# Linear attention and routed experts on one core: state products regrouped on TensorE, the state scaled on ScalarE, small routing operations on GpSimd, weights fetched at a later step

## The chip, the core and the metric

The kernel runs on one core of a Trainium2 chip. A core has five engines that run their own instruction queues in order: TensorE (PE, with weight loads shown as PEld), VectorE (DVE), ScalarE (ACT), GpSimd (POOL) and SyncE (SP), which here only issues transfers. The metric is the device time of one execution in microseconds. The kernel before took 322.28 us as the median of three runs (320.68, 322.28, 323.75).

## The reference

Two layers in a row. The first is a linear attention with a decayed state: batch 4, 8 heads, 768 positions, head size 48.

```python
def _attn_ref(q, k, v, alpha):
    state = np.zeros((B, H, D, D))
    for t in range(S):
        state = alpha[:, :, t, :, None] * state + np.einsum('bhd,bhe->bhde', k[:, :, t], v[:, :, t])
        y[:, :, t] = np.einsum('bhd,bhde->bhe', q[:, :, t], state)
```

Its output, 3072 rows of 384, goes through a mixture of 8 experts with one expert for each row:

```python
def _moe_ref(x, w_skip, w_gate, w1, w2):
    do_compute = x @ w_skip > 0
    logits = x[do_compute] @ w_gate
    e_idx = argmax(logits); gate_w = softmax(logits)[e_idx]
    for e in range(8):
        h = np.maximum(xc[e_idx == e] @ w1[e], 0.0)      # 384 -> 1024
        y[e_idx == e] = gate_w * (h @ w2[e])             # 1024 -> 384
    out[do_compute] = xc + y
```

## The kernel before

**Stage one** walks over 24 tiles of 128 positions: tile i is chunk i // 4 of batch i % 4, with all 8 heads (`static_path`, the loop at L829). In this document *step i* is one turn of that loop. Nothing reorders what the loop writes: each engine runs its instructions in the order of the Python code, and a list of small routing operations (`self.small`) is let out one at a time by `tick()` at fixed places.

Heads are held in pairs: p is the pair (0 to 3), h the half. Half 0 lies on partitions 0 to 47, half 1 on 64 to 111. A tile's work:

- `decay` (L248) for tile i+4: two scans on DVE (`sfx`, `pfx`), then three multiplications on POOL (`total`, keys by `sfx`, queries by `pfx`).
- `scores` (L270) and `causal` (L281) for tile i+1: key-query products on PE into `ps_s`, and a predicated copy by DVE into `st`. `ps_s` has one buffer, so the scores of the next step wait for this copy.
- `turn_k` (L286) for tile i+1: keys transposed on PE, copied to `kt` by ACT.
- `inter` (L296): the old state times the queries; `intra` (L324): values times `st`, added in the same PSUM tiles `ps_y`. There are two such tiles, one for each half, and two ACT copies of 48 partitions bring them to `xt`.
- `outer` (L309): the old state (by an identity product, L315) plus keys times values in `ps_v`; `carry` (L337): DVE multiplies by `total` and writes the new state, which tile i+4 reads.
- `rows` (L348) for tile i-1: PE turns `xt` to rows with the nine routing products; ACT copies `x`, DVE sums the logits.
- Routing. `route_expert` (L379) works on groups of tiles, (0,6), (6,12), (12,15), (15,18), and `route_one` on single tiles from 18 on; `route_rank` counts positions on PE, `route_slot` (L441) makes slot numbers, and `scatter` (L505) writes row numbers and gates to DRAM lists with one indirect transfer for each tile, issued by POOL.

In the same loop the weights of the first expert are fetched in eight pieces (`weight_pieces(0)` from step 3, one piece a step) and split into two parts of lower precision, twelve pieces, one a step, from step 7 (`split_pieces`, L530): ACT makes the high part, DVE or POOL (`n % 5 in (1, 3)`) the low part. The pieces of expert 1 follow from step 18.

**Stage two** runs the eight experts one after the other: gather of its 256 rows, two products with three terms each (`up`, `down`), and an indirect write of the result, while the next experts' weights are fetched and split.

Of the kernel before, what the change touches and what calls it, by code (L numbers as in the profile page):

```python
# [23 lines left out]
P = 128  # L24
# [25 lines left out]
DECAY_MIN = 1e-18  # L50
EG = 8


class Kernel:
# [130 lines left out]
    def attention_pools(self, st):  # L185
# [8 lines left out]
        self.ps_y = [st.enter_context(tc.tile_pool(name=f"ps_y{h}", bufs=1, space=PSUM)) for h in range(2)]  # L194
# [24 lines left out]
        for t in self.xtb:  # L219
            nc.scalar.copy(out=t.rearrange("p a t -> p (a t)"), in_=self.zero)  # L220
# [4 lines left out]
    def warm_up(self, n):  # L225

        ps = self.ps_y[0].tile([P, P], F32, name="ps_y")
        zero = self.nc.const_aps.tensor(0.0, [P, P], F32)
        for _ in range(n):
            self.nc.tensor.matmul(ps, lhsT=zero, rhs=zero, start=True, stop=True)  # L230
# [64 lines left out]

    def inter(self, i):  # L296


        nc, w = self.nc, self.work[i]
        w["y"] = [pool.tile([P, NP, P], F32, name="ps_y") for pool in self.ps_y]  # L300
        state = self.state[i % B][i // B % 2]
        if i // B > 0:
            for p in range(NP):
                for h in range(2):
                    r = slice(64 * h, 64 * h + D)
                    nc.tensor.matmul(w["y"][h][r, p, :], lhsT=state[r, p, :], rhs=w["qh"][r, p, :],  # L306
                                     start=(p == 0), stop=False)

    def outer(self, i):  # L309

        nc, w = self.nc, self.work[i]
        if i // B < C - 1:
            w["pv"] = self.ps_v.tile([P, NP, D], F32, name="ps_v")
            if i >= B:
                nc.tensor.matmul(w["pv"][:PD], lhsT=self.ident[:PD, :PD], rhs=self.state[i % B][i // B % 2][:PD],  # L315
                                 start=True, stop=False)
            for p in range(NP):
                for h in range(2):
                    o = (2 * p + h) * D
                    r = slice(64 * h, PD if h else 64)  # L320
# [3 lines left out]
    def intra(self, i):  # L324

        nc, w = self.nc, self.work[i]
        ps, v = w["y"], w["v"]
        for p in range(NP):
            for h in range(2):
                o = (2 * p + h) * D  # L330
                nc.tensor.matmul(ps[h][64 * h:64 * h + D, p, :], lhsT=v[:, o:o + D],  # L331
                                 rhs=w["st"][:, h, p * P:(p + 1) * P], start=(i < B and p == 0), stop=(p == NP - 1))
        xt = self.xtb[i % 2]
        for h in range(2):
            r = slice(64 * h, 64 * h + D)
            nc.scalar.copy(out=xt[r], in_=ps[h][r])  # L336
# [686 lines left out]
```

## Time and profile before

| | |
|---|---|
| median of three runs | 322.28 us |
| the profiled execution's own time | 324.01 us |
| its span, first to last instruction | 322.3 us |
| mean granted clock of TensorE | 0.936 |
| busy: PE, DVE, ACT, POOL | 291.1, 231.3, 155.1, 140.2 us |
| stage one, to the first expert's first product | about 170 us |
| stage two | about 150 us |

A profile gives, for each engine, when it was busy, and for each idle stretch what ended it. Matmuls overlap in the array, so the sum of their single times is far above the time that a group of them takes; the length of a group is read from the chain of waits or the timeline. "x16" for eight products means that each float32 product is two passes. A PE that is busy all the time may still be waiting inside, and a granted clock below 1.00 means that the array ran slower in that stretch.

### The profile page before, as it was taken

To read this page: it belongs to the slowest core of one execution; us is meant where nothing else is said; L and a number is where in the kernel's file an instruction comes from. 1 tells how busy PE (TensorE), PEld (TensorE's weight loads), DVE (VectorE), ACT (ScalarE), POOL (GpSimd) and SP (SyncE) were. 2 spreads that over 40 slices of the span, in tenths; PEclk is the share of its full clock that TensorE was granted. 3 is DMA by queue.
4 is the path that set the end of the run, shared out by engine and by line. 5 is a ranking of instruction groups with operands and counts; after the bars stand their busy time and mean duration, and the time that the engine had idled before them with its cause. 6 is when DMAs were issued, how large, how long until landed. Compare 5 with 4: busy or idle time off the path is not lost.

```text
span 322.3 us, 7348 instructions
## 1 busy us (share of the span) xinstructions
PE 291.1 (90%) x2816; PEld 269.1 (83%) x2816; DVE 231.3 (72%) x480; ACT 155.1 (48%) x300; POOL 140.2 (44%) x168
## 2 busy tenths in 40 slices
PE   5849799999999869979879889999999999999990
PEld 5748688888887758768779789999999999999990
DVE  8997757899699999975568547776676768685410
ACT  6022324345345415325525449686859596573200
POOL 5174533668965777882472522131413041221111
PEclk9575869999999999978979999999999999999997
DMA  7999899999999977743262568887885868370000
GB/s 236 288 231 158 113 219 235 241 255 221 233 164 225 252 134 153 142 82 78 81 190 60 190 250 274 280 297 248 274 297 179 315 176 287 149 258 17 19 23 24
DMA packets 28123, 60.79 MB, mean 189 GB/s; under 512 B 7110, under 2 KB 14065, under 8 KB 28080
## 3 DMA queue, kind: packets, MB, share of 16 engines
q1 hardware_dynamic: 22960, 50.43, 60.5%
q10 hardware_dynamic: 2176, 4.72, 4.8%
q0 software_dynamic: 2944, 5.09, 4.8%
q8 instruction: 24, 0.39, 0.5%
q14 instruction: 19, 0.16, 0.2%
HBM read 52.96 MB, written 8.89 MB: 192 GB/s over the span
## 4 chain that ended last, share of the span: by engine, by line
PE 75%; issue 5%; DMA 4%; POOL 4%; DVE 3%; ACT 1%; POOLq 0%; SPq 0%; DVEq 0%
PE ps_o L640 20%; PE ps_h L624 19%; PE ps_s L277 7%; PE ps_g L358 7%; PE ps_y L331 6%; PE ps_y L306 5%; PE ps_k L291 3%; PE ps_v L321 3%; DMA xr<-out_dram,meta 2%; PE ps_x L604 1%; PE ps_v L315 1%; DMA xs<-idg,slot 1%; POOL xs L508 1%; DMA meta<-xs 1%; POOL qka L268 1%
## 5 line engine op out<-in xcount | busy, mean ns | idle before, releaser
L645 POOL DMA_INDIRECT out_dram<-o,meta x16 | 16.9, 1058 | 98.8 <-DVE o L643 98.8
L277 PE MATMUL ps_s<-qka 48*128 48x128 f32 x384 | 32.6, 317 | 15.1 <-POOL qka L268 4.5
L277 PEld LDWEIGHTS ps_s<-qka 48*128 48x128 f32 x384 | 27.8, 218 | 20.4 <-issue 6.4
L640 PE MATMUL ps_o<-w2h,hh 128*128 128x384 f32 x128 | 43.8, 342 | 0.0
L336 ACT COPY xt<-ps_y 48x512 f32<-48x512 f32 x48 | 27.9, 581 | 32.1 <-PE ps_y L331 26.7
L640 PE MATMUL ps_o<-w2l,hh 128*128 128x384 f32 x128 | 43.3, 338 | 0.0
L640 PE MATMUL ps_o<-w2h,hl 128*128 128x384 f32 x128 | 43.2, 337 | 0.0
L624 PE MATMUL ps_h<-xh,w1h 128*128 128x256 f32 x192 | 33.9, 283 | 0.0
L624 PE MATMUL ps_h<-xh,w1l 128*128 128x256 f32 x192 | 33.7, 282 | 0.0
L643 DVE SCALAR_TENSOR_TENSOR o<-ps_o,meta,xr 128x384 f32<-128x384 f32 x16 | 9.9, 618 | 32.7 <-PE ps_o L640 26.6
L624 PE MATMUL ps_h<-xl,w1h 128*128 128x256 f32 x192 | 33.2, 282 | 0.0
L629 DVE SCALAR_TENSOR_TENSOR hl<-ps_h,hh 128x512 fp32r<-128x512 f32 x32 | 22.0, 688 | 14.4 <-ACT hh L628 13.0
L284 DVE COPY_PREDICATED st<-mask,ps_s 128x1024 f32<-128x1024 uint8 x24 | 31.2, 1301 | 1.2 <-PE ps_s L277 0.4
L267 POOL TENSOR_TENSOR qka<-qka,sfx 112x512 f32<-112x512 f32 x22 | 28.0, 1271 | 9.2 <-DVE sfx L257 8.9
L546 DVE TENSOR_TENSOR w2l<-raw,w2h 128x512 fp32r<-128x512 f32 x45 | 29.0, 683 | 3.1 <-ACT w2h L542 3.1
L331 PE MATMUL ps_y<-st,vt 128*48 128x128 f32 x384 | 30.6, 297 | 0.0
L358 PE MATMUL ps_g<-xw,xt 112*128 112x105 f32 x184 | 28.6, 303 | 2.1 <-ACT xt L336 2.1
L265 DVE TENSOR_TENSOR_SCAN pfx<-qka,seed 112x512 f32<-112x512 f32 x24 | 29.3, 1220 | 0.7
L546 DVE TENSOR_TENSOR w1l<-raw,w1h 128x512 fp32r<-128x512 f32 x46 | 29.7, 683 | 0.0
L628 ACT ACTIVATE hh<-ps_h 128x512 fp32r<-128x512 f32 x32 | 19.1, 595 | 21.2 <-PE ps_h L624 20.7
L257 DVE TENSOR_TENSOR_SCAN sfx<-qka,seed 112x512 f32<-112x512 f32 x24 | 29.0, 1210 | 0.3
L358 PEld LDWEIGHTS ps_g<-xw,xt 112*128 112x128 f32 x184 | 24.8, 209 | 5.3 <-ACT xt L336 2.3
(148 smaller groups left out, 621.3 us busy)
## 6 DMA issues: line engine op xcount, KB each, us to landing
raw<-in_w_dram SPq DMA_DIRECT2D x64, 384.0 KB
qka<-in_qka_dram SPq DMA_DIRECT2D x36, 288.0 KB
vt<-in_v_dram SPq DMA_DIRECT2D x24, 192.0 KB
out_dram<-x SPq DMA_DIRECT2D x24, 192.0 KB
alpha<-in_nat_dram ACTq DMA_DIRECT2D x8, 576.0 KB
qka<-in_first_dram SPq DMA_DIRECT2D x4, 672.0 KB
out_dram<-xr SPq DMA_DIRECT2D x5, 192.0 KB
qka<-in_first_dram SPq DMA_DIRECT2D x2, 448.0 KB
```

What stands on the lines that cost most here:

```text
L257: nc.vector.tensor_tensor_scan(flat(sfx)[:, ::-1], a[:, 1:SW + 1][:, ::-1], seed[:, ::-1], 0.0, ALU.mult, ALU.max)
L265: nc.vector.tensor_tensor_scan(flat(pfx), a[:, 0:SW], seed, 0.0, ALU.mult, ALU.max)
L267: pool.tensor_tensor(w["kh"][:PD], w["kh"][:PD], sfx[:PD], ALU.mult)
L277: nc.tensor.matmul(ps[:, h, p * P:(p + 1) * P], lhsT=kh[r, p, :], rhs=qh[r, p, :], start=True, stop=True)
L284: self.nc.vector.copy_predicated(w["st"], self.mask, w["ps"])
L331: nc.tensor.matmul(ps[h][64 * h:64 * h + D, p, :], lhsT=v[:, o:o + D], rhs=w["st"][:, h, p * P:(p + 1) * P], start=(i < B and p == 0), sto ...
L336: nc.scalar.copy(out=xt[r], in_=ps[h][r])
L358: nc.tensor.matmul(pg[:, p, :], lhsT=w["xt"][:PD, p, :], rhs=self.xw[:PD, p, :], start=True, stop=True)
L546: eng.tensor_tensor(lo[:, s], raw[:, s], hi[:, s].bitcast(F32), ALU.subtract)
L624: nc.tensor.matmul(ps[:, u, :], lhsT=a[:, k, f * P:(f + 1) * P], rhs=b[:, k, :], start=(n == 0), stop=(n == len(order) - 1))
L629: nc.vector.scalar_tensor_tensor(out=hl, in0=ps, scalar=0.0, in1=hh.bitcast(F32), op0=ALU.max, op1=ALU.subtract)
L640: nc.tensor.matmul(ps, lhsT=a[:, f, js], rhs=b[:, f, :], start=(n == 0), stop=(n == 3 * FT - 1))
```

## The change

- `inter` and `intra` put all heads in one PSUM tile of two banks. Bank h holds half h; within it, two pairs share columns and pair j of the two writes partitions 64j and up. The products are issued in the order (h, j) = (0,0), (1,1), (0,1), (1,0). Those of j = 0 are 64 columns wide, so that partitions 48 to 63 are written too. One ACT copy of 112 partitions replaces the two of 48. The order of heads in the inputs is rearranged to fit (`layouts`).
- `outer` issues its identity product as two, one for each half of the output.
- `carry` is four ACT multiplications of 112x48, each with its column of `total`, in place of one DVE operation.
- In `route_expert`, `d` and the multiplication by `rev` go from DVE to POOL, with one more tick behind the second; `cnt` is added up on POOL for all groups. `route_slot` makes the slots of groups on POOL.
- In the loop, `rows`, `logits` of tile i-1 and `carry` come behind `intra`, and `turn_k` runs one step earlier, at the end of step i for tile i+2.
- `weight_pieces(0)` starts at step 9 (`W0`), its split at step 12; expert 1's first four pieces are fetched at steps 18 to 21, the other four behind the loop.

```diff
+W0 = 9
...
+    HEADS = [(a, h, j) for a in range(NP // 2) for h, j in ((0, 0), (1, 1), (0, 1), (1, 0))]
+
+    def y(self, i, a, h, j):
+        m = D if j else 64
+        return m, self.work[i]["y"][64 * j:64 * j + m, h, a * P:(a + 1) * P]
...
-            for p in range(NP):
-                for h in range(2):
-                    r = slice(64 * h, 64 * h + D)
-                    nc.tensor.matmul(w["y"][h][r, p, :], lhsT=state[r, p, :], rhs=w["qh"][r, p, :],
-                                     start=(p == 0), stop=False)
+            for a, h, j in self.HEADS:
+                r, p = slice(64 * h, 64 * h + D), 2 * a + j
+                m, y = self.y(i, a, h, j)
+                nc.tensor.matmul(y, lhsT=state[r, p * D:p * D + m], rhs=w["qh"][r, p, :], start=(a == 0), stop=False)
...
-                nc.tensor.matmul(w["pv"][:PD], lhsT=self.ident[:PD, :PD], rhs=self.state[i % B][i // B % 2][:PD],
-                                 start=True, stop=False)
+                for r in part:
+                    nc.tensor.matmul(w["pv"][r], lhsT=self.ident[:PD, r], rhs=self.state[i % B][i // B % 2][:PD],
+                                     start=True, stop=False)
...
-        for h in range(2):
-            r = slice(64 * h, 64 * h + D)
-            nc.scalar.copy(out=xt[r], in_=ps[h][r])
+        nc.scalar.copy(out=xt[:PD].rearrange("p (a h) t -> p h a t", h=2),
+                       in_=w["y"][:PD, :, :2 * P].rearrange("p h (a t) -> p h a t", t=P))
...
-            nc.vector.tensor_tensor(self.state[i % B][(i // B + 1) % 2][:PD], w["pv"][:PD],
-                                    total[:PD].to_broadcast([PD, NP, D]), ALU.mult)
-            self.tick()
+            new = self.state[i % B][(i // B + 1) % 2]
+            for p in range(NP):
+                nc.scalar.mul(out=new[:PD, p, :], in_=w["pv"][:PD, p, :], mul=total[:PD, p, :])
...
+        nc.gpsimd.tensor_tensor(d, L, bc(mx), ALU.subtract)
         yield nc.vector.tensor_tensor(eq, L, bc(mx), ALU.is_equal)
-        nc.vector.tensor_tensor(d, L, bc(mx), ALU.subtract)
         nc.scalar.activation(out=ex, in_=d, func=AF.Exp)
-        yield nc.vector.tensor_tensor(eq, eq, bc(self.rev), ALU.mult)
+        yield nc.gpsimd.tensor_tensor(eq, eq, bc(self.rev), ALU.mult)
+        yield
...
-            (nc.gpsimd if g1 < SOLO else nc.vector).tensor_tensor(self.cnt[:, i + 1, :], self.cnt[:, i, :], self.m[:, i, :], ALU.add)
+            nc.gpsimd.tensor_tensor(self.cnt[:, i + 1, :], self.cnt[:, i, :], self.m[:, i, :], ALU.add)
...
-        yield nc.vector.tensor_scalar(out=self.slot[:, g0:g1, :], in0=s2, scalar1=BIG, scalar2=None, op0=ALU.add)
+        eng = nc.vector if n == 1 else nc.gpsimd
+        yield eng.tensor_scalar(out=self.slot[:, g0:g1, :], in0=s2, scalar1=BIG, scalar2=None, op0=ALU.add)
...
-                if i == 3:
+                if i == W0:
                     fetch = self.weight_pieces(0)
-                if i == 18:
+                if i == W0 + 9:
                     fetch = self.weight_pieces(1)
-                advance(fetch, 1)
+                if W0 <= i < W0 + 13:
+                    advance(fetch, 1)
...
-                if i == 7:
+                if i == W0 + 3:
                     split = self.split_pieces(0, early=True)
```

What the new order of the loop makes of the queues, at the places that the prediction speaks of. First TensorE in step 5, before (`qka_129` holds tile 6, `qka_134` tile 5, `xt_158` tile 4):

```order
L277 MATMUL ps_s<-qka_129 128x128 x8
L291 MATMUL ps_k<-ident,qka_129 128x112 x4
L306 MATMUL ps_y<-qka_134,state_153 48x128 x8
L358 MATMUL ps_g<-xw,xt_158 128x105 x4
L315 MATMUL ps_v<-state_153,ident 112x192
L321 MATMUL ps_v<-vt,kt 64x48
L321 MATMUL ps_v<-vt,kt 48x48
...
L331 MATMUL ps_y<-st_149,vt 48x128 x8
```

And TensorE in the same step of the changed kernel (`qka_126` holds tile 6, `qka_131` tile 5, `qka_127` tile 7):

```order
L276 MATMUL ps_s<-qka_126 128x128 x8
L313 MATMUL ps_y<-qka_131,state_150 64x128
L313 MATMUL ps_y<-qka_131,state_150 48x128 x2
...
L323 MATMUL ps_v<-state_150,ident 64x192
L323 MATMUL ps_v<-state_150,ident 48x192
L328 MATMUL ps_v<-vt,kt 64x48
L328 MATMUL ps_v<-vt,kt 48x48
...
L337 MATMUL ps_y<-st_146,vt 48x128 x2
...
L363 MATMUL ps_g<-xw,xt_155 128x105 x4
L290 MATMUL ps_k<-ident,qka_127 128x112 x4
```

The rows of tile 4 and the transposition, now of tile 7, stand behind the products of tile 5, and the products with the state alternate between output widths 64 and 48.

GpSimd in step 18 and at the start of step 19, before (the lists `xs` are written by the scatters, `w2l` is a piece of the split):

```order
L262 TENSOR_TENSOR total<-a_147,sfx 112x4
L267 TENSOR_TENSOR qka_133<-qka_133,sfx 112x512
L268 TENSOR_TENSOR qka_133<-qka_133,pfx 112x512
L508 DMA xs<-idg,slot 24576x2 x2
L546 TENSOR_TENSOR w2l<-raw,w2h 128x512
L262 TENSOR_TENSOR total<-a_147,sfx 112x4
L267 TENSOR_TENSOR qka_134<-qka_134,sfx 112x512
```

GpSimd at the same place of the changed kernel:

```order
L261 TENSOR_TENSOR total<-a_144,sfx 112x4
L266 TENSOR_TENSOR qka_130<-qka_130,sfx 112x512
L267 TENSOR_TENSOR qka_130<-qka_130,pfx 112x512
L515 DMA xs<-idg,slot 24576x2 x2
L553 TENSOR_TENSOR w2l<-raw,w2h 128x512
L395 TENSOR_TENSOR d<-logit,mx 128x24
L398 TENSOR_TENSOR eq<-eq,rev 128x24
L405 TENSOR_TENSOR cnt<-cnt,m 128x8 x3
L261 TENSOR_TENSOR total<-a_144,sfx 112x4
L266 TENSOR_TENSOR qka_131<-qka_131,sfx 112x512
```

The routing operations of the group (15,18) stand behind the two scatters and the piece of the split.

VectorE at the end of step 18, before, from the predicated copy of tile 19 on:

```order
L284 COPY_PREDICATED st_149<-mask,ps_s 128x1024
L344 TENSOR_TENSOR state_155<-ps_v,total 112x192
L367 TENSOR_REDUCE logit<-ps_g 128x9
L389 TENSOR_REDUCE mx<-logit 128x3
L390 TENSOR_TENSOR eq<-logit,mx 128x24
L391 TENSOR_TENSOR d<-logit,mx 128x24
L393 TENSOR_TENSOR eq<-eq,rev 128x24
L394 TENSOR_REDUCE m_1768<-eq 128x3
L395 TENSOR_TENSOR eq<-eq,m_1768 128x24
L396 SCALAR_TENSOR_TENSOR m<-logit,eq 128x24
L399 TENSOR_TENSOR cnt<-cnt,m 128x8 x3
```

And in the changed kernel, to the first scan of step 19 (the order prints scans as SCALAR_TENSOR_TENSOR):

```order
L283 COPY_PREDICATED st_145<-mask,ps_s 128x1024
L372 TENSOR_REDUCE logit<-ps_g 128x9
L394 TENSOR_REDUCE mx<-logit 128x3
L396 TENSOR_TENSOR eq<-logit,mx 128x24
L400 TENSOR_REDUCE m_1787<-eq 128x3
L401 TENSOR_TENSOR eq<-eq,m_1787 128x24
L402 SCALAR_TENSOR_TENSOR m<-logit,eq 128x24
L406 TENSOR_REDUCE s_1788<-ex 128x3
L407 TENSOR_SCALAR s_1788<-s_1788 128x3
L408 RECIPROCAL idg<-s_1788 128x3
L256 SCALAR_TENSOR_TENSOR sfx<-qka_131,seed 112x512
```

Between L396 and L400 a result of GpSimd (its L398) is now needed, where VectorE made it itself before.

53 lines of the change are left out of this document (26 added, 27 removed).

## The prediction

> **What bounds the kernel now.** I read the page first, then the windows by stage, then the chain of waits in order of time. From the page, the granted clock in 40 slices of 8.06 us, in tenths:
>
> ```profile
> PEclk9575869999999999978979999999999999999997
> ```
>
> The windows, busy time by engine with the clock behind it:
>
> ```profile
> core 0: us, PE busy (x) PEld busy (x) DVE busy (x) ACT busy (x) POOL busy (x), PEclk, DMA share, GB/s
> 46.00:67.00 21.00, 21.00 (x302) 17.72 (x302) 16.21 (x32) 8.57 (x17) 8.62 (x10) 1.00 0.97 240
> 112.00:140.00 28.00, 22.09 (x316) 18.60 (x317) 27.18 (x59) 11.00 (x22) 23.52 (x26) 1.00 0.72 140
> 140.00:160.00 20.00, 19.15 (x217) 16.11 (x218) 11.68 (x61) 7.86 (x21) 8.81 (x10) 0.83 0.37 80
> 187.00:323.00 136.00, 127.60 (x902) 126.91 (x901) 82.20 (x139) 81.51 (x149) 30.06 (x28) 0.98 0.57 195
> ```
>
> Stage one has two halves. From 46 us PE is busy all the time and DVE for 16.2 of 21 us. From 112 to 140 us DVE is full (27.2 of 28), POOL nearly (23.5), and PE idles 5.9 us. From 187 us the experts run on PE, and the change touches none of that. So it is worth its PE time only in the first half, and in the second what DVE and POOL make of it. One step of the first half in the chain, and two later starts of steps (a group of scores opens a step):
>
> ```profile
> 50.02 1.09 PE ps_s L277 x16
> 51.11 0.53 PE ps_k L291 x4
> 51.65 1.01 PE ps_y L306 x16
> 52.65 1.07 PE ps_g L358 x8
> 53.72 0.33 PE ps_v L315 x2
> 54.05 0.54 PE ps_v L321 x13
> 54.59 0.93 PE ps_y L331 x16
> 55.53 1.09 PE ps_s L277 x16
> ...
> 88.94 1.09 PE ps_s L277 x16
> ...
> 139.89 1.16 PE ps_s L277 x16
> ```
>
> A step takes 5.51 us and PE is its whole chain. DVE has slack there; it waits in each step for the state's products:
>
> ```profile
> 54.77 0.36 DVE L344 TENSOR_TENSOR state<-ps_v,total 112x192 f32<-112x192 f32 x1 [1.09 <-PE ps_v L321]
> ```
>
> In the second half one wait stands out in the timeline. `d`, an operation on 24 columns, takes 3.44 us where the same takes 0.17 later. Around it stand the first scans of steps 15 and 16 and the copy that closes step 19:
>
> ```profile
> 109.14 1.21 DVE L257 TENSOR_TENSOR_SCAN sfx<-qka,seed 112x512 f32<-112x512 f32 x1
> ...
> 113.42 1.22 DVE L257 TENSOR_TENSOR_SCAN sfx<-qka,seed 112x512 f32<-112x512 f32 x1
> ...
> 116.16 3.44 DVE L391 TENSOR_TENSOR d<-logit,mx 128x24 f32<-128x24 f32 x1
> ...
> 133.82 0.17 DVE L391 TENSOR_TENSOR d<-logit,mx 128x24 f32<-128x24 f32 x1
> ...
> 138.50 1.29 DVE L284 COPY_PREDICATED st<-mask,ps_s 128x1024 f32<-128x1024 uint8 x1
> ```
>
> It ended (119.60) as a multiplication on POOL ended (118.28 + 1.27 = 119.55):
>
> ```profile
> 118.28 1.27 POOL L268 TENSOR_TENSOR qka<-qka,pfx 112x512 f32<-112x512 f32 x1
> ```
>
> DVE waited for POOL although no data tied `d` to it. The Trainium skill (SBUF — State Buffer, "Who interferes with whom") says that a VectorE operation with two SBUF inputs and a GpSimd operation that reads SBUF exclude one another; the row agrees. By that rule the move of `d` gains its 3.4 us; it says nothing of what is queued on GpSimd.
>
> **The change part by part.** The sum is made against the profiled execution (324.0 us), then scaled to the median, 322.28. One per cent, 3.2 us, is about what a measurement tells from no change.
>
> *Products on PE.* `inter` does 16 passes in 1.01 us on two parts of the array, so one pass takes 1.01 x 2 / 16 = 0.126 us. On four parts the passes stand four deep: 4 x 0.126 = 0.51 us, a gain of 0.50. A floor is the row of `ps_v`, 16 passes of 48 columns in 0.54 us, where short passes follow one another this fast. No row shows four parts at work, so the bounds are 0 and 0.50; I take 0.45, nearest to the floor. `intra` had two column parts and keeps them: 0. The two identity products are 0.33 us if they run side by side, as the halves of L321 do, and 0.66 if not; I take 0. `rows` beside `turn_k` costs what it did; fewer changes between array shapes may give 0.05. So 5.5 becomes 5.0 us a step where PE is the chain. What is late next there: DVE's turn is 4.28 us (109.14 to 113.42), less the state's 0.36: 3.9, so PE stays the bound. Steps 4 to 11: 8 x 0.5 = **-4.0**.
>
> *ACT.* For the next terms, groups on POOL, and two others:
>
> ```profile
> L508 POOL DMA_INDIRECT xs<-idg,slot x24 | 24.2, 1009 | 7.4 <-issue 4.4 <-DVE idg L422 1.6 <-DVE sfx L257 0.3
> ...
> L262 POOL TENSOR_TENSOR total<-a,sfx 112x4 f32<-112x4 f32 x20 | 4.2, 211 | 29.0 <-DVE sfx L257 26.1 <-DVE mx L389 2.8
> L399 POOL TENSOR_TENSOR cnt<-cnt,m 128x8 bf16<-128x8 bf16 x15 | 4.2, 278 | 7.6 <-DVE m L396 6.7
> L546 POOL TENSOR_TENSOR w2l<-raw,w2h 128x512 fp32r<-128x512 f32 x3 | 3.9, 1290 | 0.1
> ```
>
> ```profile
> L546 DVE TENSOR_TENSOR w1l<-raw,w1h 128x512 fp32r<-128x512 f32 x46 | 29.7, 683 | 0.0
> ...
> L392 ACT ACTIVATE ex<-d 128x48 f32<-128x48 f32 x2 | 0.5, 243 | 5.0 <-DVE d L391 5.0
> ```
>
> Four multiplications of 48 columns cost at most 4 x 0.243 = 0.97 us a step, and one `xt` copy goes. ACT is busy 8.6 of 21 us. The next `outer` waits for the four, but scores (1.09), `turn_k` (0.53) and `inter` (0.5) stand between: 2.1 us of cover against about 1.6 (the `x` copy and the four). Taken at 0; without that cover up to 0.5 us a step. The single `xt` copy is seen in the startup only, about **-0.5** for steps 1 to 3, between 0 and 1.2.
>
> *Steps 12 to 14.* Before: 88.94 to 109.14, 20.2 us. PE now needs 5.0 a step. The split begins at step 12: its DVE pieces (0.68) and the group (6,12) bring DVE's turns to 4.6 to 5.5 us. Laid end to end, with POOL's 2.75 us for a tile (0.21 and twice 1.27) and 1.2 for a scatter (1.0 and a gap; 7.4 us of idle time stand before 24), step 15's scan comes about 18.5 us after step 12's start: **-1.7**.
>
> *Steps 15 to 19.* Before: 109.14 to 139.79, 30.65 us. With the state's operation gone a bare turn is 3.9 us; a group's eight small DVE operations cost some 0.17 each, as the unblocked `d`.
> - Step 15: 4.1 (slots on POOL, piece of the split on POOL).
> - Step 16: `m2` now waits for POOL's product with `rev`. From the end of POOL's multiplications of step 15 it does two scatters (2.4 with their gaps), a piece (1.29), `total` (0.21), `d` (0.3, as L399), two multiplications (2.54) and the product (0.3): 7.05 us. DVE does logits, two scans, `mx`, `eq` and the copy meanwhile, 4.45: a wait of 2.6. The turn is 3.9 + 0.9 + 0.68 + 0.2 + 2.6 = 8.25.
> - Step 17: 3.9 + 0.9 + 0.68 + 0.2 = 5.7.
> - Step 18: POOL has two scatters (2.4), a piece (1.29), `d` and the product (0.6) behind its multiplications, and ends these 0.8 behind DVE's copy: 5.1. DVE has 0.5 to do: a wait of 4.6. The turn is 3.9 + 1.4 + 0.2 + 4.6 = 10.1. The three `cnt` (0.83) follow on POOL; the ranking that reads them comes a step later.
> - Step 19, to the end of its copy: 3.9.
>
> The sum is 32.0, against 30.65: **+1.4**. The stalls of `d` (3.3) and of the state's operation (5 x 0.36) go, and two waits of 7.2 come. Behind the waiting `m2` stand the next decay and the next copy; PE's scores wait for that copy. The bounds are the same sum without the two waits (24.8, -5.8) and with a third wait of 4.6 (+6).
>
> *Steps 20 to 23.* Before, PE waited for two copies of `xt` in a row:
>
> ```profile
> 156.13 0.56 ACT xt L336
> 156.72 0.59 ACT xt L336
> ```
>
> Now `rows` stand between and cover it: -1.2. `inter` gains 4 x 0.45 at most: -1.8; four passes make -0.2 more. Against it, `rows` lie behind `intra`, so the ranking of a tile loses the cover of one `intra` (0.93) in three steps, up to 2.8, and two DVE pieces of the split (1.36) stand ahead of `route_one`, of which I take half. Sum **-0.5**, between -3.2 and +1.5.
>
> *Transfers.* The eight pieces come six steps later, and each is there three steps, 15 us, ahead of its split. In steps 3 to 8 the queue is lighter; no wait in the chain there is a transfer's, so 0. Two more pieces of expert 1 fall behind the loop, on SP ahead of the lists that expert 1's gather needs; 0 to 1 us, taken as **+0.3**.
>
> The sum: -0.5 - 4.0 - 1.7 + 1.4 - 0.5 + 0.3 = -5.0; 324.0 - 5.0 = 319.0, 0.985 of the profiled time, so **317 us** for the median.
>
> **The rivals.**
> - *POOL's waits are covered.* If DVE meets its product ready at steps 16 and 18, the 7.2 us of waits go: -12, 310 us. For it: an extra tick stands between product and use, and a scatter's slot may be shorter than 1.2 us. Against it: in step 18 all ticks run at once, and the order shows nothing between.
> - *Four parts don't overlap.* PE's 0.45 goes in the eleven steps 4 to 14, +5.0: 322, no change; with identity products in a row, 11 x 0.33 more, 326. For it: no row shows four. Against it: both pairings, by rows and by columns, run at full overlap in L277 and L331.
> - *Slower: POOL is late for every group.* Its work of steps 12 to 19 is eight tiles (2.75), some thirteen scatters (1.2), three pieces (1.29) and the groups' small operations (about 6), 47 us, where steps 12 to 19 last 51. Decisive point: POOL more than 4 us behind DVE when a group of step 13, 16 or 18 asks. Then each costs step 18's 4.6: 13.8 in place of 7.2, +6.6. PE idles over 4 us each time and the clock falls; the row 140:160 has 0.83 over 20 us, which is 3.4 us of work lost, and one more such stretch gives -5.0 + 6.6 + 3.4 = +5: 327 us. The Trainium skill (TensorE: Matmul & The Clock Gate, Part 1) sets the fall to half speed behind about 3.4 us without work; the clock slices of this case fall in stage one and at the very end, behind waits of PE.
>
> **How the numbers follow.** Forecast 0.46, waits covered 0.26, no overlap 0.12, POOL late 0.16. Faster by over 1% (under 319.1): all of the second case and seven tenths of the forecast's, 0.59, written 0.60. Within 1%: the rest of the forecast and most of the no-overlap case, 0.24. Slower: POOL late, 0.16. The range 309 to 326 takes in the second case, the no-overlap case with both ends, and leaves out half of POOL late.
>
> **What would show it.** Right: steps 5 to 11 at 5.0 us in the chain, with L313 x16 near 0.55; no DVE operation of a group over 0.4 us; L400 waiting for POOL in steps 16 and 18; a turn of step 18 near 10 us; the expert stage unchanged in length. Wrong: L313 near 1.0 us (no overlap), waits of ACT or of `ps_v` on PE in the first half, or idle PE and a lower clock from step 13 on (POOL late).

## The result, and the profile after

The changed kernel takes 319.33 us (median of 20 runs, 315.17 to 324.87), the kernel before in the same series 322.95 us (20 runs). The ratio is 0.9865, 95% interval 0.9824 to 0.9906: 1.35% faster, a little over what can be told from no change. The profiled execution of the changed kernel took 317.83 us with a span of 316.0 us, 6.2 us less than the profiled one of before (324.01). Single executions of every kernel here spread by about 3%, and a ratio with an interval compares only the runs near the fastest of each kernel, in two experiments from only two runs, so the medians over all runs stand beside it, and where the two disagree, nothing finer than their difference is concluded.

The granted clock in 40 slices of 7.9 us and the busy time in three windows, with the clock, the DMA share and GB/s behind them:

```profile
PEclk9655998999999999657989999999999999999998
```

```profile
46.00:67.00 21.00, 21.00 (x322) 18.31 (x320) 16.78 (x31) 7.67 (x24) 12.65 (x22) 0.92 0.88 202
112.00:140.00 28.00, 21.78 (x286) 18.33 (x279) 18.24 (x49) 8.82 (x27) 22.42 (x31) 0.80 0.50 118
140.00:160.00 20.00, 17.36 (x194) 14.94 (x193) 14.26 (x62) 8.29 (x24) 8.79 (x9) 0.85 0.21 57
```

From 112 to 140 us DVE is busy for 18.2 us where it was full (27.2 of 28), yet PE is no busier than before (21.8 for 22.1), and the clock there is 0.80 instead of 1.00. Part of DVE's stalls became waits, as the rows further down show. One step of the first half, from the chain of waits:

```profile
57.29 1.09 PE ps_s L276 x16
58.38 0.60 PE ps_y L313 x12
58.98 0.47 PE ps_v L323 x3
59.45 0.39 PE ps_v L328 x14
59.84 0.95 PE ps_y L337 x16
60.79 1.07 PE ps_g L363 x8
61.86 0.38 PE ps_k L290 x4
62.24 1.09 PE ps_s L276 x16
```

A step takes 4.95 us for 5.51, and PE is still its whole chain. The products with the state (L313) are 0.60 us for 1.01; the identity products cost 0.47 for 0.33 (two parts); the outer products 0.39 for 0.54; `turn_k`, at another place, 0.38 for 0.53.

In the second half, DVE's operations that wait, or are stalled (idle time before each in brackets, and what ended it):

```profile
92.61 0.20 DVE L400 TENSOR_REDUCE m<-eq 128x6 f32<-128x48 f32 x1 [0.45 <-POOL eq L398]
93.08 2.03 DVE L402 SCALAR_TENSOR_TENSOR m<-logit,eq 128x48 bf16<-128x48 f32 x1
...
106.23 1.22 DVE L256 TENSOR_TENSOR_SCAN sfx<-qka,seed 112x512 f32<-112x512 f32 x1 [1.65 <-issue]
...
110.88 0.18 DVE L400 TENSOR_REDUCE m<-eq 128x3 f32<-128x24 f32 x1 [0.45 <-POOL eq L398]
...
126.95 0.18 DVE L400 TENSOR_REDUCE m<-eq 128x3 f32<-128x24 f32 x1 [4.09 <-POOL eq L398]
```

For the scan at 106.23 the profile names no releaser ("issue"); in four experiments below the same scan waits too, and there the profile names the load of its tile. The last row is the wait that the prediction put at 4.6 us. POOL's queue ahead of it:

```profile
121.51 1.30 POOL L267 TENSOR_TENSOR qka<-qka,pfx 112x512 f32<-112x512 f32 x1
122.98 1.00 POOL L515 DMA_INDIRECT xs<-idg,slot  x1 [0.17 <-POOL qka L267]
124.28 0.98 POOL L515 DMA_INDIRECT xs<-idg,slot  x1 [0.30 <-issue]
125.27 1.29 POOL L553 TENSOR_TENSOR w2l<-raw,w2h 128x512 fp32r<-128x512 f32 x1
126.49 0.24 POOL L395 TENSOR_TENSOR d<-logit,mx 128x24 f32<-128x24 f32 x1
126.67 0.25 POOL L398 TENSOR_TENSOR eq<-eq,rev 128x24 f32<-128x24 f32 x1
```

Two scatters and a piece of the split stand ahead of `d` and of the product with `rev`. Behind that wait PE stands still, twice, and starts again at half speed (16 products of scores at full clock take 1.16 us):

```profile
128.17 0.17 PE L441 MATMUL ps_g<-cnt,one_b 128*128 128x24 bf16 x1 [1.99 <-POOL cnt L405]
...
132.07 2.08 PE L276 MATMUL ps_s<-qka 48*128 48x128 f32 x16 [3.70 <-DVE sl L458]
139.19 2.08 PE L276 MATMUL ps_s<-qka 48*128 48x128 f32 x16
```

The windows around it say how long: PE is busy for 13.93 of 14 us, at 0.50.

```profile
126.00:132.00 6.00, 0.38 (x5) 0.20 (x3) 4.80 (x12) 2.56 (x8) 4.11 (x9) 0.76 0.46 131
132.00:146.00 14.00, 13.93 (x118) 11.95 (x118) 6.75 (x33) 3.58 (x10) 8.04 (x9) 0.50 0.17 45
```

Where the time went, by the start of each step's scores on PE and, between the third and the fourth column, of the first scan of step 15, in us. The second pair of profiles is from the experiments below; the last two rows are the difference of the means and the forecast.

| | to step 4 | steps 4-11 | steps 12-14 | steps 15-19 | step 20 to the first expert product | experts |
|---|---|---|---|---|---|---|
| before, two profiles | 43.6, 39.0 | 45.3, 46.8 | 20.3, 21.1 | 30.8, 34.5 | 30.4, 29.5 | 152.0, 152.3 |
| changed, two profiles | 39.3, 39.1 | 42.9, 40.9 | 17.8, 17.8 | 32.1, 34.5 | 33.2, 31.0 | 150.8, 152.7 |
| difference | -2.1 | -4.1 | -2.9 | +0.7 | +2.2 | -0.4 |
| forecast | -0.5 | -4.0 | -1.7 | +1.4 | -0.5 | +0.3 |

### The profile page after: what moved, and what is told of

Its sections match the earlier page's. It is cut to its first block, busy times and chain, and to the rows that moved or that the text cites. A ratio compares the mean times of both kernels' runs of the same rounds, so it can differ in the third digit from the quotient of the medians.

```text
span 316.0 us, 7462 instructions
## 1 busy us (share of the span) xinstructions
PE 283.2 (90%) x2848; PEld 263.4 (83%) x2848; DVE 220.9 (70%) x445; ACT 153.4 (49%) x354; POOL 144.0 (46%) x183
## 4 chain that ended last, share of the span: by engine, by line
PE 60%; DVE 13%; issue 8%; DMA 7%; POOL 7%; ACT 3%; SPq 0%; POOLq 0%; DVEq 0%
PE ps_h L631 20%; PE ps_o L647 19%; DMA qka<-in_first_dram 5%; PE ps_g L363 5%; PE ps_s L276 4%; PE ps_y L337 4%; DVE sfx L256 3%; DVE pfx L264 3%; POOL xs L515 2%; PE ps_y L313 2%; DMA alpha<-in_nat_dram 2%; POOL qka L267 1%; PE ps_v L328 1%; PE ps_x L611 1%; DVE d L422 1%
## 5 line engine op out<-in xcount | busy, mean ns | idle before, releaser
L276 PE MATMUL ps_s<-qka 48*128 48x128 f32 x384 | 31.6, 310 | 15.7 <-DVE st L283 8.2
L276 PEld LDWEIGHTS ps_s<-qka 48*128 48x128 f32 x384 | 26.7, 210 | 19.9 <-POOL qka L267 7.0
L340 ACT COPY xt<-ps_y 112x512 f32<-112x512 f32 x24 | 14.0, 584 | 55.0 <-PE ps_y L337 50.2
L631 PE MATMUL ps_h<-xh,w1h 128*128 128x256 f32 x192 | 34.5, 285 | 1.1 <-DVE hl L636 1.1
L631 PE MATMUL ps_h<-xl,w1h 128*128 128x256 f32 x192 | 33.2, 282 | 0.0
L337 PE MATMUL ps_y<-st,vt 128*64 128x128 f32 (+1 forms) x384 | 32.2, 306 | 0.3 <-issue 0.2
L636 DVE SCALAR_TENSOR_TENSOR hl<-ps_h,hh 128x512 fp32r<-128x512 f32 x32 | 22.1, 689 | 14.8 <-ACT hh L635 12.7
L650 DVE SCALAR_TENSOR_TENSOR o<-ps_o,meta,xr 128x384 f32<-128x384 f32 x16 | 9.9, 617 | 30.8 <-PE ps_o L647 25.9
L635 ACT ACTIVATE hh<-ps_h 128x512 fp32r<-128x512 f32 x32 | 19.0, 595 | 22.1 <-PE ps_h L631 21.6
L631 PEld LDWEIGHTS ps_h<-xh,w1h 128*128 128x128 f32 x192 | 28.5, 192 | 1.3 <-DVE hl L636 1.3
```

Of the source, the lines that this page charges most:

```text
L276: nc.tensor.matmul(ps[:, h, p * P:(p + 1) * P], lhsT=kh[r, p, :], rhs=qh[r, p, :], start=True, stop=True)
L337: nc.tensor.matmul(y, lhsT=w["v"][:, o:o + m], rhs=w["st"][:, h, p * P:(p + 1) * P], start=(i < B and a == 0), stop=(a == NP // 2 - 1))
L631: nc.tensor.matmul(ps[:, u, :], lhsT=a[:, k, f * P:(f + 1) * P], rhs=b[:, k, :], start=(n == 0), stop=(n == len(order) - 1))
L635: nc.scalar.activation(out=hh, in_=ps, func=AF.Relu)
L636: nc.vector.scalar_tensor_tensor(out=hl, in0=ps, scalar=0.0, in1=hh.bitcast(F32), op0=ALU.max, op1=ALU.subtract)
```

## The experiments

The theory: the products on four parts are the gain; moving the group's operations traded stalls of DVE for a wait of about the same size; that wait also costs clock. The rivals are in the expectations.

**The changed kernel again**, with no edit.

> The changed kernel unaltered, so that the others stand beside it on one chip. If its profile is typical: steps 6 to 13 at 4.95 us on PE, one wait of DVE of 3.5 to 4.5 us for POOL's product with rev in the last group, half clock for some 14 us behind it, and a ratio to the kernel before of 0.980 to 0.991. If the startup gain seen in the first profile (4.3 us at the start of step 4) was chance, the starts of steps 4 to 6 come within 1 us of the kernel before's less 0.5 us a step.

Measured 317.90 us (6 runs) beside 322.77, ratio 0.9819 (0.9749 to 0.9888). Its stages are in the table. The wait in the last group was 4.08 us, the steps of the first half 4.95. Step 4 began at 39.1 us, as in the first profile.

**The kernel before again**, for the same reason.

> The kernel before unaltered, for a second profile of its stages. If the startup's loss at step 3 (8.5 us, with 3.5 us of idle PE and half clock to 45 us) and the short half clock at 141 to 148 us belong to this kernel, they come again within 1 us; if they were one execution's, step 3 takes 4.1 to 5.5 us or the loss lies in another step, and the half clock from 60 to 172 us costs between 5 and 12 us of work.

One run, 324.99 us. Step 3 took 4.0 us here, not 8.5: that loss was one execution's. Another stood at step 7 (7.5 us), and first scans of this kernel waited for loads (five, 1.2 to 1.6 us), which none did in the first profile:

```profile
51.31 1.22 DVE L257 TENSOR_TENSOR_SCAN sfx<-qka,seed 112x512 f32<-112x512 f32 x1 [1.48 <-DMA qka<-in_qka_dram]
...
81.25 1.22 DVE L257 TENSOR_TENSOR_SCAN sfx<-qka,seed 112x512 f32<-112x512 f32 x1 [1.48 <-DMA qka<-in_qka_dram]
```

So the first profile showed a kernel whose transfers were all hidden, and the second one in which they sometimes are not. Up to step 4 the changed kernel is 4.3 us ahead of the one profile of before and level with the other: no gain is shown there.

**The products alone**: the kernel before with `inter`, `outer`, `intra`, the order of heads in the layout and the single `xt` copy of the change; state, routing, weights and order as before. In short, not word for word:

```
-        self.ps_y = [pool "ps_y0", pool "ps_y1"]
+        self.ps_y = one pool, tile [P, 2, SW]
-    inter, outer, intra of before
+    inter, outer, intra of the change
```

> The kernel before with the products on four heads alone (layout, identity products in two parts, one xt copy); state scaled on VectorE, routing, weights and the order of a step as before. Theory (the first half's gain is the products, and DVE bounds the second half): inter takes 0.67 us for 1.08, steps 6 to 13 take 4.95 to 5.05 us for 5.5, steps 14 to 19 gain at most 1 us; 3 to 5 us less than the kernel before, ratio 0.985 to 0.991. Rival (the products give their time only because the state's scaling left DVE and turn_k was moved): steps stay at 5.3 to 5.5 us with PE waiting for kt or the copy, ratio 0.996 to 1.003.

Measured 318.58 us beside 322.77, ratio 0.9809 (0.9731 to 0.9888), by the medians over all runs 0.987. The whole change has 0.982 and 0.985 in the same series, so the products alone give as much as the change, within these intervals. In its profile (323.19 us, the slowest of the six runs) most steps took 5.10 us, and two (7 and 8) took 6.7 and 8.3 us, behind a late load and at half clock. The 0.15 us that are missing to 4.95 are those of `turn_k`, at its old place:

```profile
81.03 0.53 PE ps_k L291 x4
81.56 0.60 PE ps_y L311 x12
```

The stall of `d` is here as it was before:

```profile
111.41 3.44 DVE L394 TENSOR_TENSOR d<-logit,mx 128x24 f32<-128x24 f32 x1
```

The expectation gave 0.985 to 0.991: the medians lie in it, the ratio below it. Its rival (no gain without the other parts) falls.

**The last group's routing ahead of the scatters.** The same operations, in another order at step 18:

```
+                if i == SOLO:
+                    self.small = chain(self.small, self.route_expert(ends[i - 1]))
+                    self.tick(99)
...              (the step's scatters and its piece of the split)
-                if i - 1 in ends:
+                if i - 1 in ends and i != SOLO:
```

> Same operations; for the last group (tiles 15 to 17) the routing is issued ahead of the step's two scatters and of the piece of the split, no longer behind them, on POOL and DVE alike. Theory (the product waits because it stands in POOL's queue behind 3.6 us of other work, and PE's idle time behind that wait costs the clock): DVE's wait for the product falls from 4.1 to under 0.8 us, the turn of that step from 10.6 to 6.5 to 7.2 us, PE's idle time there from 5.7 to under 2, the half clock from 14 us to 7 or none; 4 to 7 us less than the changed kernel, a ratio to the kernel before of 0.965 to 0.975. Rival (POOL is full, the order doesn't matter): the scatters and the piece then hold up the next total and the multiplications with the decay, PE waits as long for its scores, and the time is within 1 us of the changed kernel, 0.983 to 0.990.

Measured 316.09 us beside 322.77: 0.979 by the medians, ratio 0.9651 (0.9549 to 0.9752) from its fastest. In its place the theory holds: the wait fell from 4.1 to 0.35 us and the step's time on PE from 10.5 to 6.8. How much of these 3.8 us shows in the time is open: 1.8 us by the medians, over 5 by the fastest runs. The profiled execution, 322.22 us, was the slowest of the six; in it DVE's next large operation ran into a stall, here with POOL's rows of the same time:

```profile
125.43 0.18 DVE L400 TENSOR_REDUCE m<-eq 128x3 f32<-128x24 f32 x1 [0.35 <-POOL eq L398]
...
130.79 3.39 DVE L553 TENSOR_TENSOR w2l<-raw,w2h 128x512 fp32r<-128x512 f32 x1
```

```profile
129.75 1.28 POOL L553 TENSOR_TENSOR w2l<-raw,w2h 128x512 fp32r<-128x512 f32 x1
130.98 0.21 POOL L261 TENSOR_TENSOR total<-a,sfx 112x4 f32<-112x4 f32 x1
131.14 1.27 POOL L266 TENSOR_TENSOR qka<-qka,sfx 112x512 f32<-112x512 f32 x1
132.36 1.26 POOL L267 TENSOR_TENSOR qka<-qka,pfx 112x512 f32<-112x512 f32 x1
133.59 0.68 POOL L461 TENSOR_SCALAR slot<-s 128x3 uint32<-128x3 f32 x1
```

A piece of the split that takes 0.68 us took 3.39: it ended at 134.18, 0.56 us behind the second multiplication (133.62), so its own work began about as that ended. In the changed kernel the same piece (132.31) came behind POOL's multiplications, since DVE was 4 us late, and met nothing. PE waited 2.1 us ahead of this and 2.6 us for what stood behind it, and half clock followed, longer than before (24 us), where the theory gave 7 or none. In this execution the wait had covered the next stall.

**Zeros in the place of PE's idle time.** 22 products of zeros into a free bank, 8 ahead of the ranking and 14 ahead of the scores behind it:

```
+        if i == SOLO:
+            self.fill(8)
         if rank:
             self.route_rank(rank, bank)
...
+                if i == SOLO + 2:
+                    self.fill(14)
                 if i + 1 < NT:
                     self.scores(i + 1)
```

> The changed kernel with 22 products of zeros (8 ahead of the ranking of tiles 15 to 17, 14 ahead of the scores behind it) in the place where TensorE idled 5.6 us; nothing else changes. Theory (that idle time starts the 14 us of half clock that follow): no half clock from 128 to 146 us, steps 20 and 21 at 4.6 to 5.5 us for 7.1, 4 to 6 us less than the changed kernel, ratio 0.967 to 0.974. Rival (the clock falls for another reason, or the stretch comes a little later anyway): within 1 us of the changed kernel or 1 to 2 us more where the zeros outlast the wait, ratio 0.980 to 0.992.

Measured 319.26 us beside 321.92, 0.992 by the medians (ratio 1.0091, 1.0040 to 1.0142): no gain, where the theory gave 0.967 to 0.974. PE's rows (the 14 products are 28 passes) and one of DVE:

```profile
126.51 3.39 PE L236 MATMUL ps_k<-const-float32-0.0 128*128 128x128 f32 x28
130.30 1.16 PE L283 MATMUL ps_s<-qka 48*128 48x128 f32 x16 [0.40 <-DVE sl L467]
...
134.26 1.16 PE L283 MATMUL ps_s<-qka 48*128 48x128 f32 x16
...
138.71 0.17 PE L451 MATMUL ps_v<-m,tri 128*128 128x8 bf16 x1 [2.56 <-DVE m L434]
```

```profile
135.77 2.89 DVE L434 SCALAR_TENSOR_TENSOR m<-rev,m,on 128x8 bf16<-128x8 f32 x1
```

The zeros end 0.4 us ahead of the scores, which run at full clock (1.16 us for 2.08), and step 20 takes 4.0 us for 7.1. So the idle time is what brought the half clock at that place, as the theory has it. Then DVE, now earlier, met a scatter, a piece of the split and one more subtraction of POOL (`latel`) in a row, an operation on 8 columns took 2.89 us, PE idled 2.56, and half clock came all the same, from 138 to 155 us: as the rival has it, the stretch came a little later.

**The group's difference and product back on VectorE.**

```
-        nc.gpsimd.tensor_tensor(d, L, bc(mx), ALU.subtract)
+        nc.vector.tensor_tensor(d, L, bc(mx), ALU.subtract)
...
-        yield nc.gpsimd.tensor_tensor(eq, eq, bc(self.rev), ALU.mult)
+        yield nc.vector.tensor_tensor(eq, eq, bc(self.rev), ALU.mult)
```

> The changed kernel with the group's difference from the maximum and the product with rev back on VectorE (slots and cnt stay on GpSimd). Theory (moving them traded stalls for waits of the same size): DVE's waits for GpSimd's product (0.45, 0.45 and 4.1 us) go; instead d or the product on VectorE are blocked by GpSimd's multiplications for 1.3 to 3.5 us in at least one of the three groups; within 2.5 us of the changed kernel, ratio 0.975 to 0.990. Rival (the move was worth its 3.4 us or more): slower than the changed kernel by 3 us, ratio 0.991 to 0.998.

Measured 315.31 us beside 321.92, 0.979 by the medians (ratio 0.9862, 0.9734 to 0.9990): no slower than the changed kernel, as far as six runs tell. The waits are gone, and the stalls that should have come back were small, 0.90 us at most in a group:

```profile
106.16 1.22 DVE L256 TENSOR_TENSOR_SCAN sfx<-qka,seed 112x512 f32<-112x512 f32 x1 [3.39 <-DMA qka<-in_qka_dram]
...
122.81 0.90 DVE L395 TENSOR_TENSOR d<-logit,mx 128x24 f32<-128x24 f32 x1
```

So no run shows a gain from that move; by the interval alone one of up to 1% is not excluded. The first row shows something else: a scan waited 3.4 us for its load. It also made the group of step 16 late, so that `d` came behind POOL's piece of the split; that the stalls were small here is in part this accident.

**The state on VectorE.** One multiplication by `total` on DVE in place of the four on ScalarE, at the same place.

> The changed kernel with the state scaled by one VectorE operation at the same place, in place of four on ScalarE. Theory: first half unchanged, 4.95 us a step, since PE is the chain and DVE has slack; 0.36 us more in each of some six steps of the second half, +1 to +2.5 us, ratio 0.985 to 0.994. Rival (the operation in VectorE's queue waits for the outer products and holds up the decay, and GpSimd's multiplications block it): steps 6 to 12 at 5.1 us or more and over 4 us in all, ratio 0.995 to 1.005.

Measured 319.98 us beside 321.92, 0.994 by the medians (ratio 1.0080, 1.0006 to 1.0154). Steps of the first half stayed at 4.95 us, and up to the first expert product it is level with the changed kernel (164.3 us for 165.3 and 163.4); what its profile has more lies in the experts (154.6 us), which the edit leaves alone. The ratio is 2% above the changed kernel's and the medians 0.5 to 1%, but the changed kernel did not run in this series, and the profile shows no cost ahead of the experts: what the state's place is worth stays open.

**The weights early**: loads from step 3, split from step 7, as in the kernel before.

```
-                if i == W0:           (9)
+                if i == 3:
...
-                if i == W0 + 3:
+                if i == 7:
```

> The changed kernel with the first expert's weights loaded from step 3 and split from step 7, the second's from step 18, as in the kernel before. Theory (moving the weights is worth nothing in the first half, and costs in the last steps, where pieces of the split now stand on DVE and ACT ahead of route_one): steps 6 to 13 stay at 4.95 us; steps 20 to 23 get 0.7 to 1.5 us shorter; within 1.5 us of the changed kernel, rather faster. Rival (early weights compete with the loads of q, k and v and of the startup): steps 3 to 8 wait for loads and are 2 to 5 us longer in all, ratio 0.992 to 1.003.

Measured 318.47 us beside 322.77, 0.987 by the medians (ratio 0.9857, 0.9790 to 0.9923): as the changed kernel. Both sides were right about a place: steps 4 to 11 took 44.6 us for 42.9 and 40.9, with scans waiting for loads, the longest 1.78 us,

```profile
47.70 1.22 DVE L255 TENSOR_TENSOR_SCAN sfx<-qka,seed 112x512 f32<-112x512 f32 x1 [1.78 <-DMA qka<-in_qka_dram]
```

and step 20 to the first expert product took 27.7 for 33.2 and 31.0. No pieces of the split stood there, and the half clock behind the same wait of step 18 (4.09 us) was short, 6.8 us; this run does not separate the two. It also shows step 16 with a scan that did not wait for its load, and there the wait for POOL's product is long:

```profile
107.04 1.22 DVE L255 TENSOR_TENSOR_SCAN sfx<-qka,seed 112x512 f32<-112x512 f32 x1
...
113.37 0.18 DVE L399 TENSOR_REDUCE m<-eq 128x3 f32<-128x24 f32 x1 [2.21 <-POOL eq L397]
```

**The group first and the weights early**, loads from step 5 and the split from step 7.

> The last group's routing ahead of the scatters (as in the run that put it first), and the first expert's weights loaded from step 5 and split from step 7, so that the split is done at step 18. Theory (with the wait for the product gone, the next thing late was a VectorE piece of the split of 3.39 us, blocked by GpSimd's multiplications with the decay at step 19, and PE's idle time behind it): no piece of the split and no wait over 0.8 us on DVE after step 18, the turn of step 18 at 6.5 to 7.2 us, from step 20's start to the first expert product 25.5 to 28 us for 33.2 and 31.1; 5 to 9 us less than the changed kernel, ratio to the kernel before 0.956 to 0.968. Rival (the loads and VectorE pieces in the first half cost as much as they give at the end, as with early weights alone): steps 6 to 12 at 5.2 us or more in the mean, ratio 0.972 to 0.985.

Measured 313.90 us beside 321.92, 0.975 by the medians (ratio 0.9796, 0.9707 to 0.9885): both in the rival's range. The split was done at step 18, but step 20 to the first expert product took 34.1 us in the profile, where the theory gave 25.5 to 28, and at step 19 an operation with one tensor of 8 columns was stalled in its stead (on 128 rows, usually 0.16 us):

```profile
128.86 2.68 DVE L419 TENSOR_SCALAR on<-logit 128x8 f32<-128x8 f32 x1
```

In steps 9 to 13 five scans waited 0.3 to 1.0 us for their loads, and these steps took 5.4 us in the mean, as the rival has it.

**The weights spread**: the group's operations on VectorE as above, and the first expert's weights in 12 pieces of 256 KB, one in each of steps 6 to 17, split from step 8.

```
-W0 = 9
+W0 = 6
...
-                    fetch = self.weight_pieces(0)
+                    fetch = self.weight_pieces(0, parts=6)
...
-                if i == W0 + 3:
+                if i == 8:
```

> The kernel with the group's routing on VectorE, and besides the first expert's weights in 12 pieces of two thirds the size, one in each of steps 6 to 17 (before: 8 in steps 9 to 16), split from step 8. Theory (with steps of 4.95 us the loads of q, k and v share the queues with a weight piece and come late: first scans waited 1.1 to 3.4 us for them in steps 15 to 17 of five runs, none in the kernel before): no first scan after step 6 waits over 0.8 us for a load, steps 15 and 16 together 10.5 to 12 us for 13.2 in the run with the group on VectorE; no piece of the split behind step 19; 3 to 6 us less than that run, ratio to the kernel before 0.960 to 0.972. Rival (the waits come from the transfers of the cleared lists at step 14, not from the weights): waits of 1 to 3 us stay in steps 15 to 17, ratio 0.974 to 0.985.

Measured 313.33 us beside 325.30, 0.963 by the medians (ratio 0.9732, 0.9629 to 0.9834). Step 20 to the first expert product: 27.1 us. One wait for a load stayed, at step 16 (1.57 us), and it points to the rival (the profiles so far show such waits at steps 15 to 17 in four runs, not five):

```profile
103.03 1.22 DVE L256 TENSOR_TENSOR_SCAN sfx<-qka,seed 112x512 f32<-112x512 f32 x1 [1.57 <-issue]
```

**All pieces of the split on VectorE**, besides.

> The same, with all twelve pieces of the split on VectorE (five were on GpSimd). Theory (a piece on GpSimd blocks VectorE's small operations for 1 to 2 us and stands ahead of the scatters; VectorE has the time in the first half): no VectorE operation of a group or of route_one over 1 us in steps 12 to 19, steps 8 to 14 at 4.95 to 5.1 us, 0 to 2.5 us less than the run with pieces on both, ratio 0.955 to 0.970. Rival (0.68 us more in five steps puts VectorE at the end of the step): steps 13, 15 and 18 are 0.5 us longer and nothing is gained, ratio 0.968 to 0.978.

Measured 317.30 us (8 runs) beside 325.30, 0.975 by the medians (ratio 0.9669, 0.9545 to 0.9792). No small operation of a group was stalled over 1 us, as expected; the wait at step 16 was 2.59 us here. Against the run before, the median is 4.0 us longer and the ratio lower, and the two intervals overlap: these runs decide nothing between the two ways to split.

**The late rows cleared later.** The weights spread, and the five writes of zeros moved from step 14 to step 19:

```
-                if i == 14:
+                if i == 19:
                     self.clear_late()
```

> The kernel with the group's routing on VectorE and the weights spread, and the five writes of zeros to the late rows (196 KB each) moved from step 14 to step 19, behind the last load. Theory (the first scan of step 16, which waited 1.6 and 2.6 us for its load in the two runs with spread weights, waits behind these writes, which stand ahead of that load in SyncE's queue; not behind the weights): that wait falls under 0.4 us, step 16 takes 5.4 to 6.0 us for 7.0 and 8.0, the rest of the first stage is unchanged; 1 to 3 us less than the spread weights alone, ratio to the kernel before 0.955 to 0.970. Rival (load and weight piece together are what is late): the wait stays over 1 us, and the time within 1 us, ratio 0.966 to 0.980.

Measured 310.61 us beside 322.92, 0.962 by the medians (ratio 0.9744, 0.9677 to 0.9811); all six runs lie between 307.3 and 311.6. The scan of step 16 no longer waits,

```profile
102.89 1.21 DVE L256 TENSOR_TENSOR_SCAN sfx<-qka,seed 112x512 f32<-112x512 f32 x1
```

and step 16 takes 5.3 us for 7.0 and 8.0. So the wait does not come without the writes. It does not come without the weight pieces either: in both runs with early weights the writes stood at step 14, no weight piece stood beside them, and that scan did not wait (step 15, by the scans, 4.6 us). As far as these profiles show, it takes both in the queue. This kernel has the lowest median of all here, and its interval lies below the changed kernel's of 20 runs (0.9824 to 0.9906): steps 15 to 19 (by the scores) take 29.4 us for 32.9 and 35.3 in the changed kernel, step 20 to the first expert product 26.4 for 33.2 and 31.0, and the half clock there lasts some 4 us. That it is faster than the spread weights alone is not shown: 2.7 us by the medians, nothing by the ratios (0.9744 and 0.9732), and the ratios of two other experiments are lower.

## Why the prediction was right, and where it was not

The time (317 forecast, 319.3 measured; ratio 0.984 and 0.9865) and the sign came out, and the likeliest case was the one that happened. Not all steps did, and that the total came out so close is in part luck: the misses of steps 12 to 14, of the startup and of steps 20 to 23 offset one another.

- **Products on four parts: right.** 0.55 us a step for 0.5, and steps 4 to 11 gave 4.1 us for 4.0 (2.4 and 5.9 in the two pairs of profiles, so the closeness of the mean is chance). The four parts overlap (0.60 us, bounds 0.51 and 1.01). The identity products don't run side by side for nothing: +0.14 us, taken as 0; the outer products and `turn_k` gave 0.15 each, taken as 0 and at most 0.05 together; the 0.15 of `turn_k` come with its new place, as the run of the products alone shows, which has the other terms and no less of a gain. The rival of no overlap falls.
- **Steps 12 to 14: right in sign, small in size**, -2.4 and -3.3 us for -1.7. The sum laid the stage out at 18.5 us, and both profiles have 17.8; which term of it was too long is open.
- **The wait of step 18: right**, 4.09 and 4.08 us for 4.6, turns of 10.55 and 10.54 us for 10.1 (first scan to first scan). The order of POOL's queue was its cause, as the run with the group first shows.
- **The wait of step 16: wrong**, 0.45 and 0.30 us for 2.6. The sum let POOL start behind its scatters and piece with DVE on time. DVE was late itself: its scan waited 1.65 us for a load in one profile, and `eq` was stalled for 2.0 us in the other. So step 15 took 6.25 and 6.13 us for 4.1, step 16 took 5.78 and 7.28 for 8.25, and the stage came out at +0.7 for +1.4 (+1.3 and 0.0 in the two pairs) by errors that cancel. Where DVE was on time, in the two runs with early weights, it did wait 2.21 us: the mechanism was right, its condition was not met.
- **"No DVE operation of a group over 0.4 us": wrong.** `m` (L402) took 2.0 us behind a scatter and POOL's piece of the split in both profiles, and 1.9 to 2.0 us in every experiment that left `d` and the product on POOL and a piece of the split at that place. The move took two operations out of the way of such a stall and left others in it (`eq`, `m`). The reading of `d` as a stall that goes was right; that this is worth 3.3 us no run shows: with `d` back on VectorE the kernel is no slower, as far as six runs tell.
- **Transfers, "0": wrong, as a step.** It asked whether the weights come in time for their split, not whether the loads of q, k and v still come in time when a step is 0.55 us shorter and a weight piece or the cleared rows stand in the same queue. No scan waited in the first profile of before; in the faster kernels they wait, up to 3.4 us, where weight pieces and cleared rows meet; the second profile of before has such waits too, so one profile was not enough to take them as 0.
- **Steps 20 to 23, "-0.5": wrong sign, +2.2.** The term had the copies and the pieces of the split, not the clock. PE's 5.7 us of idle time behind the wait of step 18 brought half clock while PE worked again, 14 us in one profile and some 7 in the other; the zeros in its place took that stretch away. The prediction gave such a fall of the clock only to the rival in which POOL is late for every group; one wait is enough. So a part of that rival's price came in with the forecast. In all, half clock fills 16.1 and 10.5 us of this stage in the changed kernel, 10.2 and 3.4 in the kernel before; an estimate from that, at half speed, is 3.3 us more of lost work, so the rest of the term, near -1, was not far off. Its written parts (-3.2, up to +2.8, and half of 1.36) give between -2.5 and +0.3; -0.5 was a choice between them, and the upper bound of +1.5 lies beyond them.
- **Startup**: the 2.1 us seen are no more than the spread of one execution.

At step 20 the changed kernel was about 8 us ahead (132 us for 139.9 and 141.4), 2 of them from the startup, and 2 us were given back in the last steps.

## What to carry over

When the bound engine gets faster, price the loads again: bytes per step by the new step, with everything else in their queue. An operation moved to another engine waits behind all that stands in that queue, so its place in the order can matter more than its engine; here the same operations, issued ahead of 3.5 us of other work and not behind it, took the wait away (4.1 to 0.35 us). A stall or wait that is removed may have been the cover of the next one: in three of the runs that took the wait of step 18 or PE's idle time behind it away (the group first, with and without early weights, and the zeros), the profile shows another VectorE operation held up, for 2.7 to 3.4 us.

## What the runs showed of the hardware

- A VectorE operation that meets GpSimd can wait through a whole run of GpSimd's operations, not only through one: 3.39 us through the end of a piece, `total` and two multiplications (129.75 to 133.62), 3.44 us for `d` through four operations of the same kind. The Trainium skill (SBUF — State Buffer, "Who interferes with whom") has an operation with two SBUF inputs contend with GpSimd's reads, and lets whoever issues first, in VectorE's two-port modes, hold the shared pair of ports for the whole instruction. The trace shows more: the waiting side is passed over between instructions that follow one another closely. Operations with a single tensor of 8 or 3 columns (TENSOR_SCALAR) are hit too, 2.68 us with the group first and the weights early, 1.93 us in the run that cleared the late rows later. The same section counts `tensor_scalar` among the operations that can take the pair. VectorE's scans read two tensors as well, but only one of them lies in SBUF (`seed` is a PSUM tile in the kernel), and they are not hit: all in the fourteen profiles take 1.20 to 1.23 us, and the one that begins at 129.45 us in the changed kernel takes 1.22 us while POOL multiplies from 129.43 to 130.69. What decides whether an operation is caught stays open: of 170 VectorE operations on at most 48 columns with both inputs in SBUF that began during a scatter, in the first 170 us of the fourteen profiles, 18 took over 0.8 us.
- Half clock outlasts its cause, and by very different lengths. Behind the same 5.7 us of idle TensorE it lasted 17.1 us in the changed kernel (14 of them work, 132 to 146 us, above), 10.2 in its second profile and 6.8 with the weights early; around waits of 2.1 and 2.6 us, in the run with the group first, 23.9, of which these 22 are work:

```profile
135.00:157.00 22.00, 21.97 (x181) 18.53 (x181) 11.52 (x53) 7.86 (x20) 8.66 (x9) 0.50 0.18 37
```

In the granted clock of all fourteen profiles every stretch of half clock, but for the one that the program's end cuts off, is a multiple of 3.41 us long, from 3.4 to 23.9: what such a stretch costs jumps from run to run, and one profile doesn't price it. The Trainium skill (TensorE: Matmul & The Clock Gate, Part 1) has the clock come back after about 3.4 us of sustained work. These rows don't agree: TensorE was busy for 13.93 of 14 and for 21.97 of 22 us at 0.50; why, no run here shows. Products of zeros in the idle time kept the clock at full speed.
